# Scores and X on 32-row pieces of the array, float32 work kept together, and fewer, wider warming matmuls in an attention and two-MLP kernel

## The chip, the cores and the metric

One core of one Trainium2 chip runs the whole program. The metric is the device time of one execution in microseconds (us), the median of several runs. TensorE (PE) does the matmuls; VectorE (DVE), ScalarE (ACT) and GpSimd (POOL) do the rest; SyncE (SP) issues the DMAs. PE writes its results to PSUM, eight banks of 128 partitions x 512 float32 words.

## The reference

Four batches of eight heads, 576 tokens, 64 columns a head; the kernel unpacks the MLP weights, which come as 64-bit floats:

```python
q_lm = q.reshape(B, H, 32, 18, 64).mean(axis=3)      # 32 landmarks a head
k_lm = k.reshape(B, H, 32, 18, 64).mean(axis=3)
A  = sm(q, k_lm)          # softmax(a b^T / 8), 576 x 32
Bm = sm(q_lm, k_lm)       # 32 x 32
C  = sm(q_lm, k)          # 32 x 576
Z  = Bm^T / (norms of Bm)
for _ in range(6):
    Z = 2 * Z - Z @ Bm @ Z
x = A @ Z @ C @ v         # all heads side by side: 2304 tokens x 512
xn = x / rms(x) * rms_g
x = (silu(xn @ w_gate) * (xn @ w_val)) @ w_out       # 512 -> 1536 -> 512
out = (s * relu(x @ w_in)**2 + b) @ w_out2           # 512 -> 2048 -> 512
```

## The kernel before

**Stages.** Batch 0's attention runs first, with little beside it. Then the first MLP runs batch by batch in 12 units (blocks of 128 hidden columns, two halves of 288 tokens), and beside the units of one batch the attention of the next is computed. After the last unit and the remaining output products comes the second MLP in five blocks of up to 512 tokens.

**Precision.** The MLPs split each float32 operand into a float32r value and its remainder and add three float32r products (`PART3`; L1072, L1118, L1182, L1208 are their matmuls). The attention multiplies in float32, which leaves two records a matmul in the trace, with one exception: in batches 2 and 3 (`b >= FINE`) the scores of C and A are products of three float32r matmuls too (L707). For these, `halve` (L489) splits the transposed k or q (1152 columns) and the landmark means on ACT or DVE and DVE or POOL.

**Attention of one batch.** Heads are taken four at a time, group g = 0 or 1, a head to 32 partitions. Landmark means are sums on POOL or DVE; in batches 2 and 3 DVE transposes 32x32 blocks (L566, L596) and a product with a mask makes a block-diagonal operand of 128 columns for the four heads (L570), so that scores are matmuls over all 128 rows. Batches 0 and 1 transpose on PE (L587) and compute the scores per head on 64x32 pieces of the array (L720). `b_mm` (L620 or L615) computes B; L645 (`diag`) holds the steps of the inverse on 32x32 pieces; `c_side` and `a_side` hold the softmaxes. C's softmax finds the maximum over both halves of the row, then takes the exponentials of each (L739, L750, L755). L772 transposes C's exponentials, L794 multiplies with v. `W` = Z C v per head is written with a mask into a block operand (L859), and X = A W is computed only for the row norms: per half and group two matmuls over 64 rows each (L898), and four squares on ACT (L904). The normalised A goes to the first MLP as split operand (L944 to L950); the MLP's first weights are multiplied with W beforehand (`fused`, L1091).

**Order.** A planner written out in Python (`Scheduler`) gives every operation a due time, `key`, and lays each engine's order out from estimated durations; engines then work strictly in that order. On PE an operation has a mode, "f" or "r" (float32r); once the MLP has begun, due times in the other mode are shifted by `HOLD` or `FETCH` (L197), and a change of mode is charged (`TO_F`, `TO_R`). A batch's attention is spread by `by_path` between the times of `at_time` (L1271): from the first unit of the batch before to `EARLY` = 15 us ahead of its own first unit.

**Buffers.** PSUM banks 0 to 3 gather the output products; banks 4 to 7 (`gv_r`) serve the hidden products, and attention after batch 0 uses banks 6 and 7 of them (`at_r`). A `Buf` holds its slot from its first operation to its last.

**Warming.** Until 60 planned us, idle planned time of PE is filled with bf16 matmuls on ones, 256 columns into bank 7 (L1395), one for each `WCOST` = 0.125 us.

Of the kernel before, what the change touches and what calls it, by code (L numbers as in the profile page):

```python
# [7 lines left out]
F32 = mybir.dt.float32  # L8
# [16 lines left out]
WCOST = 0.125  # L25
FINE = 2
# [11 lines left out]
BMM = 0.15  # L38
XC = 2.0
# [9 lines left out]
HOLD, FETCH = 2.0, 4.0  # L49
AHEAD_TO, AHEAD, AHEAD_KEY = 45, 0.5, 3  # L50
# [48 lines left out]
class Scheduler:  # L99
# [48 lines left out]
    def start_of(self, o, e):  # L148
        t = max((f + (self.SAME if d == e else PEC if e == 'pe' and o.key > 5 else self.CROSS) for d, f in o.ready.items()), default=0.0)
# [17 lines left out]
    def run(self, warm):  # L167
# [8 lines left out]
        steady = False  # L176
        while left:
# [87 lines left out]
def t_act(n):  # L265
    return 0.055 + 0.00085 * n
# [15 lines left out]
def tile_nystrom_attention_two_mlps(  # L282
# [28 lines left out]
    S_ = Scheduler({"pe": nc.tensor, "dve": nc.vector, "act": nc.scalar, "pool": nc.gpsimd, "sp": nc.sync})  # L311
# [19 lines left out]
    mask4 = sb.tile([128, 1, 4, 1], F32, name="mask4")  # L331
# [30 lines left out]
    R_COLS = 15104  # L362
# [14 lines left out]
    eC_r = rring(1, 576)  # L377
# [3 lines left out]
    bd_r = rring(4, 256)  # L381
# [41 lines left out]
    def consts(_):  # L423
        nc.vector.memset(ones, 1.0)
        nc.vector.memset(spare, 1.0)
        nc.vector.memset(mask4, 0.0)
        nc.vector.memset(mask2, 0.0)
        nc.vector.memset(mask1, 0.0)
        for h in range(4):
            nc.vector.memset(mask4[32 * h:32 * h + 32, :, h, :], 1.0 / SEG)  # L430
# [26 lines left out]
    def attention(b, t0, t1):  # L457
        first = b == 0
        slow = COLD if first else 1.0
        fine = b >= FINE  # L460
        part3 = ((0, 0), (0, 1), (1, 0))
# [18 lines left out]
        area = {"t": (0, SEG * D), "bd": (SEG * D, 256)}  # L480

        def part(i, nm):
            c0, n = area[nm]
            return pair[i].t.rearrange("p k n -> p (k n)")[:, c0:c0 + n]

        def named(nm):
            return [(pair[i], nm) for i in range(2)]

        def halve(nm, x, r, n):  # L489

            wh, wl = named(nm)
            at({"act": t_act(n), "dve": t_dve2(n)}, 0, lambda e: (
                e.activation(out=part(0, nm), in_=x(), func=ACTF.Copy) if e is nc.scalar
                else e.tensor_copy(out=part(0, nm), in_=x())), r=r, w=[wh], pair=True)
            at(dp(n), 0, lambda e: e.tensor_tensor(
                out=part(1, nm), in0=x(), in1=part(0, nm).bitcast(F32), op=ALU.subtract), r=[*r, wh], w=[wl])

        src = {}
        for nm, a in (("k", k), ("q", q)):
            for g in range(2):  # L500
                t = src[nm, g] = Buf(qk_r[nm, g])

                def load_heads(e, t=t, a=a, g=g):
# [5 lines left out]
                    for h in range(4):  # L509
                        e.dma_start(  # L510
                            out=t.t[32 * h:32 * h + 32].rearrange("p (t d) -> p t d", d=D),
# [22 lines left out]
        for i, (nm, g) in enumerate((("k", 0), ("k", 1), ("q", 0), ("q", 1))):  # L534
# [19 lines left out]
            if not fine:  # L554
# [14 lines left out]
            d = bd[nm, g] = Buf(bd_r)  # L569
            at(dp(256), pos, lambda e, l=l, d=d: e.tensor_tensor(  # L570
                out=d.t.rearrange("p (e h i) -> p e h i", e=2, h=4),
                in0=l.t.rearrange("p (e o i) -> p e o i", e=2, o=1).to_broadcast([128, 2, 4, 32]),
                in1=mask4.to_broadcast([128, 2, 4, 32]), op=ALU.mult), r=[l, "const"], w=[d])

        def bdv(x):
            return x.t.rearrange("p (e m) -> p e m", e=2)

        def transposed(nm, g, pos):
# [29 lines left out]
        pB = Buf(ps_r)  # L608

        def b_mm(_):  # L610
            for g in range(2):
                if not fine:
                    for h in range(4):
                        i, p = loaded(g, h)
                        nc.tensor.matmul(  # L615
                            out=pB.t[32 * h:32 * h + 32, 32 * g:32 * g + 32], lhsT=bd["q", i].t[0:D, p],
                            rhs=bd["k", i].t[0:D, p], start=True, stop=True)
# [11 lines left out]
        def c2(x):  # L629
# [5 lines left out]
        at(("dve", t_dve(64)), pos, lambda e: e.tensor_reduce(out=bm.t[:, 0:2], in_=v2(pB), axis=AX, op=ALU.max), r=[pB], w=[bm])  # L635
        at(("dve", t_dve(64)), pos, lambda e: e.tensor_tensor(
            out=v2(Bs), in0=v2(pB), in1=c2(bm).to_broadcast([128, 2, 32]), op=ALU.subtract), r=[pB, bm], w=[Bs])
        at(("act", t_act(64)), pos, lambda e: e.activation(out=Bs.t, in_=Bs.t, func=ACTF.Exp, scale=scale / SEG if fine else scale), r=[Bs], w=[Bs])
# [62 lines left out]
        def scores(ps, nm, g, hf, p0, r, w):  # L701
            other = "kq"[nm == "k"]
            if fine:
                def mm(_):
                    for e in range(2):
                        for k, (u, y) in enumerate(part3):
                            nc.tensor.matmul(  # L707
                                out=ps.t[:, 0:HC], lhsT=part(u, "bd")[:, 128 * e:128 * e + 128],
                                rhs=part(y, "t").rearrange("p (t e i) -> p t e i", e=2, i=32)[
                                    :, HB * hf:HB * hf + HB, e, :],  # L710
                                start=(e == 0 and k == 0), stop=(e == 1 and k == 2))

                at(("pe", 6 * t_mm(HC)), p0 + 0.02, mm, r=[*named("t"), *named("bd"), *r], w=[ps, *w])
                mine[-1].mode = "r"
                return
# [11 lines left out]

        Cv = Buf(cv_r)

        def c_side(g, p0):  # L730
            for j in (g,) if fine else (0, 1) if g == 0 else ():
                transposed("k", j, p0)
# [10 lines left out]
            def in_order(hf):  # L743
                x = eC.t[:, 0:S]
                if fine:
                    return x.rearrange("p (i n) -> p n i", i=M)[:, HB * hf:HB * hf + HB]
# [18 lines left out]
            at(("dve", 0.5), p0 + 0.05, c_rec, r=[(cs, 0), (cs, 1)], w=[rc])  # L765
            pE = [Buf(ps_r), Buf(ps_r)]
# [23 lines left out]
            def cv_mm(_):  # L790
# [10 lines left out]
                e.activation(out=Cv.t[:, D * g:D * g + D], in_=pV.t[:, 0:D], func=ACTF.Copy, scale=rc.t[:, 0:1])  # L801
                if e is nc.scalar else e.tensor_scalar(
                    out=Cv.t[:, D * g:D * g + D], in0=pV.t[:, 0:D], scalar1=rc.t[:, 0:1], scalar2=None, op0=ALU.mult)),
# [3 lines left out]

        def a_side(hf, g, p0):
            if hf == 0:
                for j in (g,) if fine else (0, 1) if g == 0 else ():  # L810
                    transposed("q", j, p0)
            pA, A, a = Buf(ps_r), Buf(a_ring), Buf(AT_r)
# [10 lines left out]
            n_mine = len(mine)  # L823
# [608 lines left out]
```

## Time and profile before

| | us |
|---|---|
| median of 3 runs (lowest, highest) | 859.71 (858.71, 860.39) |
| the profiled execution's own time | 861.0 |
| its span, first to last instruction | 859.3 |
| PE busy | 843.6 |
| DVE busy | 658.2 |
| ACT busy | 460.6 |
| POOL busy | 130.0 |

Busy time is the union of an engine's instructions; matmuls overlap in the records, and their ends are modelled, so that the pace of PE is read from one start to the next. A row of the timeline gives start, duration, engine, line, tile names, shape (rows*columns of the array, then partitions x columns of the moving operand) and count.

### The profile page before, as it was taken

The page shows a single profiled execution, that of the slowest core. Times are in us where ns is not written, and L with a number is a line of the kernel's source. Part 1 is how long each engine was busy: PE and PEld are TensorE (multiplying, and loading weights), DVE is VectorE, ACT ScalarE, POOL GpSimd, SP SyncE. Part 2 cuts the span into 40 slices and gives each one's busy share as a digit, 9 for nine tenths or more (in the row PEclk, how much of TensorE's full clock was granted, in tenths as well). Part 3 has the DMA queues.
Part 4 walks back from the last instruction along what each step waited for, and adds up shares of the span by engine and source line. Part 5 has one row for each costly group of instructions (what it writes and reads, how often), then busy time and mean ns, then how long its engine had stood idle before and what let it go on. Part 6 is the DMA issues. An engine that isn't in the chain of part 4 may idle for free.

```text
span 859.3 us, 16086 instructions
## 1 busy us (share of the span) xinstructions
PE 843.6 (98%) x6039; PEld 691.4 (80%) x6039; DVE 658.2 (77%) x1492; ACT 460.6 (54%) x969; POOL 130.0 (15%) x185
## 2 busy tenths in 40 slices
PE   8899999999999999999999999999999999999997
PEld 6578776888788877888888888888888888888886
DVE  7787998889897896789978866766676667666686
ACT  5698979544544455698826633433343334333454
POOL 0270064714660143000000000000000000000000
PEclk9799999999999999999999999999999999999999
DMA  9989879644242422587732100100010001000100
GB/s 289 313 291 354 274 229 299 190 125 118 74 148 87 136 67 72 168 293 257 236 114 60 64 0 1 50 0 1 1 50 0 1 1 44 6 1 1 35 16 24
DMA packets 66493, 96.46 MB, mean 112 GB/s; under 512 B 24176, under 2 KB 44656, under 8 KB 66416
## 3 DMA queue, kind: packets, MB, share of 16 engines
q1 hardware_dynamic: 66224, 95.18, 34.9%
q8 instruction: 47, 0.77, 0.4%
q14 instruction: 30, 0.25, 0.1%
q10 hardware_dynamic: 192, 0.26, 0.1%
HBM read 81.27 MB, written 14.16 MB: 111 GB/s over the span
## 4 chain that ended last, share of the span: by engine, by line
PE 90%; DVE 4%; ACT 3%; issue 1%; DMA 0%; POOL 0%; DVEq 0%; ACTq 0%; POOLq 0%
PE bank L1208 23%; PE bank L1072 23%; PE bank L1118 17%; PE bank L1182 16%; PE bank L1091 3%; PE bank L1164 2%; PE bank L707 1%; PE bank L898 1%; PE bank L645 1%; PE bank L1395 1%; PE bank L938 1%; ACT cmag L1007 0%; DMA region<-in_k_dram 0%; PE bank L720 0%; PE bank L794 0%
## 5 line engine op out<-in xcount | busy, mean ns | idle before, releaser
L1072 PE MATMUL bank<-xh,uh 128*128 128x512 f32 (+1 forms) x320 | 119.1, 372 | 0.0
L1373 ACT ACTIVATE hbuf<-bank 128x512 f32<-128x512 f32 (+1 forms) x78 | 43.2, 553 | 141.5 <-PE bank L1072 141.4
L1072 PE MATMUL bank<-xh,ul 128*128 128x512 f32 (+1 forms) x320 | 118.8, 371 | 0.0
L1072 PE MATMUL bank<-xl,uh 128*128 128x512 f32 (+1 forms) x320 | 117.6, 368 | 0.0
L1208 PE MATMUL bank<-wh,hh 128*128 128x512 f32 x288 | 114.4, 397 | 0.3 <-DVE hh L967 0.3
L1208 PE MATMUL bank<-wl,hh 128*128 128x512 f32 x288 | 113.8, 395 | 0.0
L1208 PE MATMUL bank<-wh,hl 128*128 128x512 f32 x288 | 113.6, 395 | 0.0
L1182 PE MATMUL bank<-hh,wh 128*128 128x512 f32 (+1 forms) x224 | 87.1, 389 | 0.0
L1182 PE MATMUL bank<-hh,wl 128*128 128x512 f32 (+1 forms) x224 | 83.1, 371 | 0.0
L1182 PE MATMUL bank<-hl,wh 128*128 128x512 f32 (+1 forms) x224 | 83.0, 371 | 0.0
L968 DVE TENSOR_TENSOR hl<-hbuf,hh 128x512 fp32r<-128x512 f32 (+8 forms) x125 | 69.5, 560 | 2.8 <-ACT hh L966 0.3
L1072 PEld LDWEIGHTS bank<-xl,uh 128*128 128x128 f32 x320 | 60.3, 188 | 12.2
L1072 PEld LDWEIGHTS bank<-xh,uh 128*128 128x128 f32 x320 | 60.1, 188 | 11.5
L966 ACT ACTIVATE wh<-region 128x512 fp32r<-128x512 f32 x51 | 32.2, 631 | 69.1 <-PE bank L1208 67.9
L1072 PEld LDWEIGHTS bank<-xh,ul 128*128 128x128 f32 x320 | 60.1, 188 | 11.2
L967 DVE CAST uh<-region 128x512 fp32r<-128x512 f32 x57 | 24.3, 426 | 54.0 <-PE bank L1072 54.0
L1208 PEld LDWEIGHTS bank<-wh,hl 128*128 128x128 f32 x288 | 54.4, 189 | 13.2 <-DVE hl L968 0.2
L968 DVE TENSOR_TENSOR wl<-region,wh 128x512 fp32r<-128x512 f32 x70 | 48.5, 692 | 20.0 <-ACT wh L966 19.3
L1208 PEld LDWEIGHTS bank<-wh,hh 128*128 128x128 f32 x288 | 54.2, 188 | 11.7 <-DVE hh L967 0.7
L1208 PEld LDWEIGHTS bank<-wl,hh 128*128 128x128 f32 x288 | 54.4, 189 | 11.1
L1118 PE MATMUL bank<-xh,uh 128*128 128x288 f32 x200 | 60.7, 303 | 0.7 <-DVE hbuf L1137 0.7
L1118 PE MATMUL bank<-xl,uh 128*128 128x288 f32 x200 | 59.0, 295 | 0.0
(226 smaller groups left out, 1960.4 us busy)
## 6 DMA issues: line engine op xcount, KB each, us to landing
rawg<-keptg SPq DMA_DIRECT2D x36, 512.0 KB, 4.4
stage<-in_moe_w_out_dram SPq DMA_DIRECT2D x28, 512.0 KB, 4.8
rawo<-kepto SPq DMA_DIRECT2D x48, 256.0 KB, 2.7
stage<-in_moe_w_in_dram SPq DMA_DIRECT2D x16, 512.0 KB, 4.9
keptg<-rawg SPq DMA_DIRECT2D x12, 512.0 KB, 5.0
xbuf<-in_moe_w_val_dram SPq DMA_DIRECT2D x10, 512.0 KB, 7.4
xbuf<-in_moe_w_gate_dram SPq DMA_DIRECT2D x9, 512.0 KB, 7.0
region<-in_v_dram SPq DMA_DIRECT2D x16, 256.0 KB, 4.7
```

What stands on the lines that cost most here:

```text
L645: nc.tensor.matmul(out=ps.t[p, pn * g:pn * g + n], lhsT=lhsT(p, g), rhs=rhs(p, g), start=True, stop=True)
L707: nc.tensor.matmul(out=ps.t[:, 0:HC], lhsT=part(u, "bd")[:, 128 * e:128 * e + 128], rhs=part(y, "t").rearrange("p (t e i) -> p t e i", e=2 ...
L966: e.activation(out=hi(), in_=src(), func=ACTF.Copy) if e is nc.scalar
L967: else e.tensor_copy(out=hi(), in_=src())), r=r, w=[wh], pair=True)
L968: b = op({"dve": t_dve(n), "pool": t_pool(n)}, key, lambda e: e.tensor_tensor(out=lo(), in0=src(), in1=hi().bitcast(F32), op=ALU.subtract) ...
L1072: nc.tensor.matmul(out=ps.t[:, 0:n], lhsT=w[a].t[:, ks], rhs=x[y].t[:, kd, 0:n], start=(kd == 0 and i == 0), stop=(kd == KD - 1 and i == 2))
L1091: nc.tensor.matmul(out=pU[g].t[m, 256 * j:256 * j + 256], lhsT=gw[b].t[p, m], rhs=r.t[p, :, 128 * k:128 * k + 128], start=True, stop=True)
L1118: nc.tensor.matmul(out=ps.t[:, 0:HC], lhsT=u[a].t[:, 256 * g + 128 * part:256 * g + 128 * part + 128], rhs=x[y].t.rearrange("p k n -> p (k ...
L1164: nc.tensor.matmul(out=A[c].t[:, d:d + m], lhsT=r.t[:, 128 * c:128 * c + 128], rhs=h.t[:, o:o + m], start=f == 0 and d == 0, stop=False)
L1182: nc.tensor.matmul(out=A[c].t[:, 0:n], lhsT=w[a].t[:, 128 * c:128 * c + 128], rhs=hs[y].t[:, 0:n], start=(f == 0 and i == 0), stop=(f == F ...
L1208: nc.tensor.matmul(out=A[c].t, lhsT=hs[a].t[:, s], rhs=w[y].t, start=(f == 0 and i == 0), stop=(f == F2 - 1 and i == 2))
L1373: e.activation(out=r.t[:, 0:n], in_=ps.t[:, 0:n], func=ACTF.Relu) if e is nc.scalar
```

## The change

Scores of batches 2 and 3 (`scores2`, `c_both`, `a_side`): a call now covers both head groups of one half, with 16 float32 matmuls of 32 rows by 32 columns, two (e = 0, 1) on each of eight pieces; group 1's heads are loaded two places further round (`piece`), so that the two groups use different pieces, and each group writes its own bank. `halve` and the block-diagonal operands are gone. For k a half is 16 of the 32 segments with all their 18 tokens, not nine tokens of every segment; C's exponentials use each half's own maximum and are scaled to the common one afterwards (`fit`, one more exponential of four columns). B is computed on 32x32 pieces too, into two banks.

X of batches 1 to 3 (`XB = 1`): one call per half with eight float32 matmuls of 32 rows by 64 columns into four banks from `gv_r`; steps on a made-up engine "hold" take these banks in the planner, as each comes free, ahead of the call, and the second half's wait for the first half's call. W is copied without mask.

Planner: after a return to "r" PE stays with it for `DWELL` = 2.5 us if such work is ready (from 145 us on); attention is due 25 us instead of 15 ahead of its first unit, and that of batches 2 and 3 may begin 30 us earlier. Warming matmuls stream 512 columns (the ones read twice), one per 0.25 us.

```diff
-WCOST = 0.125
+WCOST = 0.25
+XB = 1
+SCORE2 = 1.02
+DWELL, DWELL_FROM = 2.5, 145
...
+            if e == "pe" and mode == "r" and at < since + DWELL and at > DWELL_FROM:
+                kept_r = [(t, o) for t, o in ready if o.mode == "r"]
+                if kept_r and min(t for t, _ in kept_r) <= at + self.SOON:
+                    ready = kept_r
...
                 if steady and o.mode != mode:
                     at = max(at, free[e] + (TO_R if o.mode == "r" else TO_F))
+                    since = at
...
-    eC_r = rring(1, 576)
+    eC_r = rring(2, 576)
-    bd_r = rring(4, 256)
+    bd_r = rring(4, 128)
...
+        unit = scale / SEG if b >= FINE else scale
...
+        def piece(g, h):
+
+            r = 32 * ((h + 2 * g) % 4)
+            return slice(r, r + 32)
...
-            d = bd[nm, g] = Buf(bd_r)
-            at(dp(256), pos, lambda e, l=l, d=d: e.tensor_tensor(
-                out=d.t.rearrange("p (e h i) -> p e h i", e=2, h=4),
...
-            if fine:
-                d = bd["kq"[nm == "k"], g]
-                halve("t", lambda: t.t, [t], SEG * D)
-                halve("bd", lambda: d.t, [d], 256)
...
                 for e in range(2):
-                    nc.tensor.matmul(
-                        out=pB.t[:, 32 * g:32 * g + 32], lhsT=bdv(bd["q", g])[:, e],
-                        rhs=lmT["k", g].t[:, 32 * e:32 * e + 32], start=(e == 0), stop=(e == 1))
-
-        at(("pe", 0.8 if fine else BMM), 0.18, b_mm, r=[*bd.values(), *[x for n, x in lmT.items() if n[0] == "k"]], w=[pB])
+                    for h in range(4):
+                        p, x = piece(g, h), slice(32 * e, 32 * e + 32)
+                        nc.tensor.matmul(
+                            out=pB[g].t[32 * h:32 * h + 32, 32 * g:32 * g + 32], lhsT=lmT["q", g].t[p, x],
+                            rhs=lmT["k", g].t[p, x], start=(e == 0), stop=(e == 1))
...
-            if fine:
-                def mm(_):
-                    for e in range(2):
-                        for k, (u, y) in enumerate(part3):
-                            nc.tensor.matmul(
-                                out=ps.t[:, 0:HC], lhsT=part(u, "bd")[:, 128 * e:128 * e + 128],
-                                rhs=part(y, "t").rearrange("p (t e i) -> p t e i", e=2, i=32)[
-                                    :, HB * hf:HB * hf + HB, e, :],
-                                start=(e == 0 and k == 0), stop=(e == 1 and k == 2))
...
+        def scores2(ps, nm, hf, p0, r=(), w=()):
+            other = "kq"[nm == "k"]
+
+            def mm(_):
+                for e in range(2):
+                    for g in range(2):
+                        x = tt[nm, g].t.rearrange("p (t e i) -> p t e i", e=2, i=32)
+                        x = x[:, :, e, 16 * hf:16 * hf + 16] if nm == "k" else x[:, HB * hf:HB * hf + HB, e, :]
+                        for h in range(4):
+                            p = piece(g, h)
+                            nc.tensor.matmul(
+                                out=ps[g].t[32 * h:32 * h + 32, 0:HC], lhsT=lmT[other, g].t[p, 32 * e:32 * e + 32],
+                                rhs=x[p], start=(e == 0), stop=(e == 1))
+
+            at(("pe", SCORE2), p0 + 0.02, mm, r=[*[lmT[other, g] for g in range(2)], *[tt[nm, g] for g in range(2)], *r],
+               w=[*ps, *w])
...
+        def c_both(p0):
...
+                pC = [Buf(ps_r), Buf(ps_r)]
+                scores2(pC, "k", hf, p0, [], [(x, "taken") for x in eC] if hf == 0 else [])
...
+            if fine and g == 0:
+                pA2[hf] = [Buf(ps_r), Buf(ps_r)]
+                scores2(pA2[hf], "q", hf, p0)
...
+            if b >= XB:
+                e.tensor_copy(out=WBD.t[:, 0:2 * D], in_=pW.t[:, 0:2 * D])
+                return
...
+            if b >= XB:
+                pX = [Buf(any_r if first else gv_r) for _ in range(KD)]
+                for x in pX:
+                    at(("hold", 0.0), p0, lambda e: None,
+                       r=[WBD, AT[hf, 0], AT[hf, 1]] + ([("xm", b)] if hf else []), w=[(x, "taken")])
+
+                def x_mm(_, pX=pX, hf=hf):
+                    for g in range(2):
+                        for h in range(KD):
+                            p = slice(32 * h, 32 * h + 32)
+                            nc.tensor.matmul(
+                                out=pX[h].t[D * g:D * g + D, 0:HC], lhsT=WBD.t[p, D * g:D * g + D],
+                                rhs=AT[hf, g].t[p, 0:HC], start=True, stop=True)
+
+                at(("pe", 0.65), p0, x_mm, r=[WBD, AT[hf, 0], AT[hf, 1], *[(x, "taken") for x in pX]],
+                   w=[*pX, (xq, "taken"), ("xm", b)])
...
-    EARLY = 15
+    EARLY, LEAD_B = 25, 30
...
-        return T[F1 * (b - 1)], T[F1 * b] - EARLY
+        return T[F1 * (b - 1)] - (LEAD_B if b > 1 else 0), T[F1 * b] - EARLY
...
         nc.tensor.matmul(
-            out=banks[7].t[:, 0:256], lhsT=ones.bitcast(BF16)[:, 0:128], rhs=ones.bitcast(BF16),
-            start=True, stop=True)
+            out=banks[7].t, lhsT=ones.bitcast(BF16)[:, 0:128],
+            rhs=ones.bitcast(BF16).unsqueeze(1).to_broadcast([128, 2, 256]), start=True, stop=True)
```

## Rows read from the trace of the kernel before

**Rows 1.** The page, part 1 (busy us, share, instructions) and part 3 (queue: packets, MB, share).

```profile
PE 843.6 (98%) x6039; PEld 691.4 (80%) x6039; DVE 658.2 (77%) x1492; ACT 460.6 (54%) x969; POOL 130.0 (15%) x185
...
q8 instruction: 47, 0.77, 0.4%
```

**Rows 2.** Busy time by stage: length, engines (instructions), granted clock, DMA share, GB/s.

```profile
25.00:35.00 10.00, 8.05 (x104) 4.89 (x105) 6.42 (x22) 2.93 (x8) 2.68 (x4) 0.66 1.04 372
...
55.00:420.00 365.00, 362.26 (x3392) 297.52 (x3391) 311.92 (x787) 241.17 (x557) 115.90 (x161) 1.00 0.58 188
420.00:855.00 435.00, 434.69 (x2057) 361.10 (x2055) 305.55 (x565) 182.82 (x330) 0.25 (x1) 1.00 0.09 27
```

**Rows 3.** Waits of PE: total us, times, longest.

```profile
PE bank L645 <- issue: 2.5, 1, 2.5
```

**Rows 4.** Chain that ended last, 40 to 72 us: start, us, what.

```profile
45.46 0.80 ACT cmag L1015
...
54.77 6.55 PE bank L1118 x48
```

**Rows 5.** Old scores of batches 2, 3: timeline (start, us), then one of three groups.

```profile
171.58 0.29 PE L707 MATMUL bank<-xh 128*128 128x288 f32 x1
...
172.39 0.29 PE L1118 MATMUL bank<-xh 128*128 128x288 f32 x1
...
L707 PE MATMUL bank<-xh 128*128 128x288 f32 x32 | 9.9, 311 | 0.2
```

**Rows 6.** Timeline of PE: scores of batches 0 and 1 on 64x32 pieces.

```profile
13.04 1.35 PE L720 MATMUL bank<-region 64*32 64x288 f32 x32
14.02 0.86 PE L720 MATMUL bank<-xbuf,region 64*32 64x288 f32 x16
...
98.94 0.83 PE L720 MATMUL bank<-region 64*32 64x288 f32 x16
99.70 0.50 PE L1182 MATMUL bank<-hh,wh 128*128 128x512 f32 x1
```

**Rows 7.** Timeline of PE: one call of X; group of all calls from 42 us on.

```profile
224.82 0.29 PE L1118 MATMUL bank<-xh,ul 128*128 128x288 f32 x1
225.04 0.76 PE L898 MATMUL bank<-region 64*128 64x288 f32 x4
225.72 0.40 PE L1118 MATMUL bank<-xh,uh 128*128 128x288 f32 x1
225.96 0.30 PE L1118 MATMUL bank<-xl,uh 128*128 128x288 f32 x1
226.10 0.29 PE L1118 MATMUL bank<-xh,ul 128*128 128x288 f32 x1
...
L898 PE MATMUL bank<-region 64*128 64x288 f32 x48 | 9.1, 455 | 0.0
```

**Rows 8.** Timeline of PE: B of batch 2; a short stay in the MLP.

```profile
178.88 1.08 PE L620 MATMUL bank<-region 128*128 128x32 f32 x8
...
204.39 0.33 PE L645 MATMUL bank<-region 32*32 32x32 f32 x16
204.65 0.50 PE L1182 MATMUL bank<-hh,wh 128*128 128x512 f32 x1
...
206.15 0.71 PE L772 MATMUL bank<-ident,region 128*128 128x128 f32 x5
```

**Rows 9.** ACT's work on X and on halving: min/median/max ns; then count, busy us.

```profile
L904 ACT ACTIVATE region<-bank x32: 387/408/485, 34.6 to 325.8; 128x288 f32<-128x288 f32 x32
...
L493 ACT ACTIVATE xh<-region 128x1152 fp32r<-128x1152 f32 (+1 forms) x9 | 8.9, 999 | 9.4 <-PE bank L707 8.4 <-POOL region L570 0.5 <-PE bank L1118 0.4
```

**Rows 10.** Timeline of PE: steps of batch 0's inverse with warming between.

```profile
27.96 0.65 PE L645 MATMUL bank<-region 32*32 32x64 f32 x16
28.55 1.03 PE L1395 MATMUL bank<-ones 128*128 128x256 bf16 x4
29.51 0.65 PE L645 MATMUL bank<-region 32*32 32x64 f32 x16
```

More of the change, by code (lines that the diff above doesn't have):

```diff
@@ L148, in start_of @@
     def start_of(self, o, e):
-        t = max((f + (self.SAME if d == e else PEC if e == 'pe' and o.key > 5 else self.CROSS) for d, f in o.ready.items()), default=0.0)
+        t = max((f + (0.0 if d == "hold" else self.SAME if d == e else PEC if e == 'pe' and o.key > 5 else self.CROSS) for d, f in o.ready.items()), default=0.0)
         t = max(t, o.after, self.ports if e in o.pair else 0.0)
@@ L309, in tile_nystrom_attention_two_mlps @@
     scale = 1.0 / float(D) ** 0.5
[L311 removed]
+    S_ = Scheduler({"pe": nc.tensor, "dve": nc.vector, "act": nc.scalar, "pool": nc.gpsimd, "sp": nc.sync, "hold": None})
     op = S_.op
@@ L479, in attention, with part @@
         pair = xs[1, b] = (Buf(x_r[0]), Buf(x_r[1]))
[L480 to L496, printed above, removed]
+        def part(i):
+            return pair[i].t.rearrange("p k n -> p (k n)")[:, 0:SEG * D]
+        def piece(g, h):
+            r = 32 * ((h + 2 * g) % 4)
+            return slice(r, r + 32)
         src = {}
@@ L510, in load_heads @@
                         e.dma_start(
-                            out=t.t[32 * h:32 * h + 32].rearrange("p (t d) -> p t d", d=D),
+                            out=t.t[piece(g, h)].rearrange("p (t d) -> p t d", d=D),
                             in_=a[b, 2 * h + g].rearrange("(i t) d -> i t d", t=SEG))
@@ L634, in attention, with b_max @@
         bm, bs, st, stT, nrm = (Buf(sm_r) for _ in range(5))
[L635 to L638, printed above, removed]
+        def b_max(e):
+            for g, x in enumerate(pB):
+                c = slice(g, g + 1) if fine else slice(0, 2)
+                e.tensor_reduce(out=bm.t[:, c], in_=v2(x)[:, c], axis=AX, op=ALU.max)
+                e.tensor_tensor(out=v2(Bs)[:, c], in0=v2(x)[:, c], in1=c2(bm)[:, c].to_broadcast(
+                    [128, 1 if fine else 2, 32]), op=ALU.subtract)
+        at(("dve", (0.4 if fine else 0.16) + t_dve(64)), pos, b_max, r=pB, w=[bm, Bs])
+        at(("act", t_act(64)), pos, lambda e: e.activation(out=Bs.t, in_=Bs.t, func=ACTF.Exp, scale=unit / SEG if fine else unit), r=[Bs], w=[Bs])
         at(("dve", t_dve(64)), pos, lambda e: e.tensor_reduce(out=bs.t[:, 0:2], in_=v2(Bs), axis=AX, op=ALU.add), r=[Bs], w=[bs])
@@ L730, in c_side @@
         def c_side(g, p0):
-            for j in (g,) if fine else (0, 1) if g == 0 else ():
-                transposed("k", j, p0)
+            if g == 0:
+                for j in range(2):
+                    transposed("k", j, p0)
             pC = [Buf(ps_r), Buf(ps_r)]
@@ L822, in a_side @@
             bc = [128, HB, 32]
-            n_mine = len(mine)
-            scores(pA, "q", g, hf, p0, [], [(A, "taken")])
+            if not fine:
+                scores(pA, "q", g, hf, p0, [], [(A, "taken")])
             at(("dve", t_dve(HC)), p0 + 0.03, lambda e: e.transpose(out=a3(A), in_=a3(pA)), r=[pA], w=[A])
@@ L888, in attention @@
             n_mine = len(mine)
-            for c in range(KD):
+            if b >= XB:
[4 more added lines that the diff above has]
+                def x_mm(_, pX=pX, hf=hf):
+                    for g in range(2):
+                        for h in range(KD):
[5 more added lines that the diff above has]
+                   w=[*pX, (xq, "taken"), ("xm", b)])
+                for c in range(KD):
+                    at(("act", t_act(HC)), p0 + 0.01, lambda e, c=c, pX=pX, xq=xq: e.activation(
+                        out=xq.t[:, HC * c:HC * c + HC], in_=pX[c].t[:, 0:HC], func=ACTF.Square), r=[pX[c]], w=[(xq, c)])
+            for c in range(0 if b >= XB else KD):
                 g, pr = divmod(c, 2)
@@ L954, in attention @@
                     at(("pool", 0.1), p0 + 0.11, lambda e, cols=cols: e.tensor_copy(
-                        out=mark, in_=part(1, "t")[:, cols][:, 0:1].bitcast(F32)), r=wl, w=["sums"])
+                        out=mark, in_=part(1)[:, cols][:, 0:1].bitcast(F32)), r=wl, w=["sums"])
             if hf:
```

104 lines of the change are left out of this document (71 added, 33 removed).

## The prediction

> **What bounds the kernel now.** I read the page first, then busy time by stage, then the waits of TensorE (PE), then PE's instructions in order of time. The page shows PE busy for 843.6 of 859.3 us [rows 1]. By stage the picture splits in three [rows 2]. From 420 us to the end PE is busy for 434.7 of 435 us with the second MLP, which the change does not touch: zero there. From 55 to 420 us, where the attention of batches 1 to 3 runs beside the first MLP, PE is busy 362.3 of 365 us, with VectorE (DVE) at 311.9 and ScalarE (ACT) at 241.2: a microsecond of PE work taken out here is a microsecond of time, unless a new wait appears. Before 55 us the attention of batch 0 is a chain through all engines; PE is also held 2.5 us by something that the profile calls issue [rows 3], and the granted clock averages 0.66 from 25 to 35 us, a mix of the levels 2.4 and 1.2 GHz [rows 2]. From 43 to 54 us the chain of waits lies for most of its time on ACT's unpacking of weights, and from 54.77 us on PE [rows 4].
>
> Busy times of matmuls overlap, so I price PE work by start to start.
>
> **Scores of batches 2 and 3.** Before, a call is six float32r matmuls of 288 columns on the whole array: the first starts at 171.58, the next operation's at 172.39, so 0.81 us, with no loss at either end, as the MLP uses the same mode [rows 5]. 3 x 32 matmuls [rows 5] are 16 calls: 13.0 us. After, there are 8 calls (k and q, two halves, two batches) of 16 float32 matmuls on 32x32 pieces, two per piece, on 8 different pieces. A float32 matmul leaves two records, so a call is 32 records. The trace has no such piece with 288 columns; the nearest rows are batch 0's scores on 64x32 pieces, where 8 pieces are also in use: 32 records take 13.04 to 14.02, 0.98 us [rows 6]. Inside a run of float32 work I take that. Alone, a call costs more: 16 records of the same kind that stand alone take 98.94 to 99.70, 0.76, against 0.49 inside a run, so 0.27 for the drain; and entering and leaving cost 0.08 and 0.10 (below). Alone 1.43, beside other float32 work 0.98. Half of the calls each way: 9.6 us, so **-3.4** (bounds: all beside -5.2, all alone -1.6; if only four pieces ran at a time, 0.98 more per call, +6.3).
>
> **X of batches 1 to 3.** Before, 48 records in fours are 12 calls [rows 7]. One alone: 225.04 to 225.72, 0.68; the matmul ahead of it holds PE 0.22 instead of 0.14, the first behind it 0.24 instead of 0.14: 0.86 in all [rows 7]. 12 of them: 10.3 us. After, 6 calls of 16 records on 8 pieces of 32x64. Nearest again the 16 records on 8 pieces: 0.76 alone, with 0.18 at the ends 0.94; 5.6 us, so **-4.7** (bounds: 0.49 each inside a run -7.4; four pieces at a time -1.8). The new call writes four PSUM banks, taken from the four that the first MLP uses, where the old one took two; see the first rival.
>
> **B of batches 2 and 3.** 8 records on the whole array, 1.08 us at most, become 32 on 32x32 pieces, at 0.33 for 16 [rows 8]: **-0.8** for two (bounds 0 and -1.2).
>
> **Gathering.** From 145 us on, the planner now stays with float32r work for 2.5 us after a return, as long as some is ready. In the timeline I count 40 runs of float32 work from 145 to 420 us. One alone, the 16 records of 204.39, holds PE 0.26 us, and the next starts at 206.15 after 1.5 us of MLP [rows 8]; seven runs begin less than 2.5 us behind another, apart from X's. Merging two saves the 0.18 at the ends and a drain of some 0.15 to 0.27. Four merged: **-1.4** (bounds 0 and -3).
> The Trainium skill, "TensorEngine Tiling (Array Packing)", section Tiling Modes, says that changing the tiling mode drains TensorE. It speaks against this change, which takes scores that ran in the MLP's mode out of it; the trace agrees (0.27 of drain and 0.18 at the ends), and with it every lone score call comes out at 1.43, not 0.98, which is the lower gain of 1.6 above.
>
> **Warming and the start.** 103 warming matmuls become about half as many with twice the columns, the same streaming time; where a gap has room for an odd number, one fewer. They lie on the path: between two steps of the inverse, four of them hold PE from 28.55 to 29.51, where the clock is half granted [rows 10]; the new ones would hold it as long. What can change is the 2.5 us of issue: PE stops in the middle of 16 pairs while waiting for no engine, and 6039 matmuls with as many weight loads over 47 packets of queue q8 [rows 1] are 257 per packet, so I read it as PE waiting for its code. With half the warming, some 26 pairs fewer stand ahead of it, and the shortage comes later or shorter. Bounds: +1 (two longer warming matmuls in front of a due step, at half clock), -5 (stall gone, 2.5, and the clock back for four steps of the inverse, each with half of its 0.96 of warming and some 0.1 of its matmuls, 2.3). ACT's unpacking behind it takes part of any gain [rows 4]. I take **-1.0**.
>
> **Other engines.** Gone are the halvings of k and q and of their means (ACT's casts alone 8.9 us [rows 9], and as many subtractions on DVE and GpSimd (POOL)) and the products with the block mask; new are four scalings of C per batch, one reduce, one scale and an exponential of four columns. The sum falls. Beside a PE that is the bound this is worth 0; if PE waited for this chain, it would be a gain. Attention is due 10 us earlier and may begin 30 us earlier; its loads are the same DMAs on SP's queue, which were hidden: 0.
> **New waits.** A's scores now take both attention banks at once, where a call took one and the other stayed open for the next; and PE works in order, so behind a score or X call that waits stands the MLP. For places where the new order makes PE wait I add **+1.0** (bounds 0 and +15, by the first rival).
>
> Sum: -3.4 - 4.7 - 0.8 - 1.4 - 1.0 + 1.0 = -10.3. The profiled execution took 861.0 us (span 859.3), so 850.7; the median of the runs, 859.7, is 1.3 lower: **849.4 us**.
>
> **Rivals.**
> 1. X starves the first MLP (slower). From the moment the weights are ready the new hold steps seize all four banks of the hidden layer, and the second half of the batch does the same behind the first. Until a call has run (0.94) and two squares (0.41 each [rows 9]) have freed two banks, with about 1 us of seizing ahead, no hidden matmul can run: 2.8 us. Against it: the output matmuls use other banks, and one step of them is 12 x 0.25 = 3 us [rows 8], usually ready. If none is ready, 6 x 2.8 = 17 on the sum without its +1.0: 865. It decides against the change from an idle time of 11.3 / 6 = 1.9 us per call.
> [...]
> 2. Only four pieces run side by side: +6.3 for the scores, -1.8 for X, B 0, the rest as above: +3.1, 862.8. Rows 6 speak against it, but with 64-row pieces.
> 3. Nothing is gathered: scores all alone (-1.6) and no run fewer (0): -7.1, 852.6. The count of float32 runs would show it.
> 4. The code stall and the low clock go altogether: 4 more, 845.4.
> 5. The waiting for float32r work strings out the attention chain, and PE stands at the start of batches 2 and 3, 3 us each: 855.4. Against it: the chain is given 10 us more lead.
>
> **Chances.** Forecast 0.52 (its own range 846 to 852), rivals 0.10, 0.04, 0.14, 0.12, 0.08. The range that leaves out 2 in 10 runs from 844.5 to 857.5. A measurement here can tell 0.2%, 1.7 us, from none. Faster by more: forecast and rivals 3 to 5 less their tails, 0.84; slower: rivals 1 and 2 less theirs, 0.11; within: 0.05.
>
> **What would show it.** Right: one call of the new scores at 1.0 to 1.45 us start to start and X at 0.5 to 0.95; fewer than 40 float32 runs between 145 us and the end of the first MLP; that end about 10 us earlier; the second MLP as long as before. Wrong: PE idle beside X with its squares as releaser (rival 1); records of a call at 60 ns apart (rival 2); a PE wait at a batch's first hidden matmul (rival 5). A start phase that is shorter by more than 2 us would mean rival 4; one that is longer by more than 1 us, that my reading of the warming is wrong.

## The result, and the profile after

The changed kernel takes **851.85 us** (median of 6 runs, 850.33 to 853.25) against 858.59 for the kernel before on the same chip: a ratio of 0.9915, 95% interval 0.9898 to 0.9932. The profiled execution took 850.33 us, its span is 848.6. Forecast were 849.4, between 844.5 and 857.5. The time falls as forecast; several terms of the sum, and the idea that they add, don't hold.

The page of the changed kernel, parts 1 and 3, to compare with [rows 1]: PE is busy 12.3 us less, the span is 10.7 shorter.

```profile
PE 831.3 (98%) x6241; PEld 670.5 (79%) x6241; DVE 648.2 (76%) x1469; ACT 454.8 (54%) x971; POOL 118.3 (14%) x172
...
q8 instruction: 49, 0.80, 0.4%
```

Busy time by stage, after, with the columns of [rows 2] and borders moved by the 10.5 us by which the second MLP starts earlier (433.2 before, 422.7 after). The clock from 25 to 35 us is full instead of 0.66 (in a second profile of the same kernel, r2, it is 0.66 from 25 to 30 us and full from there); the middle still leaves PE 3.7 us without work; the last stage is as it was.

```profile
25.00:35.00 10.00, 8.45 (x118) 4.20 (x117) 9.53 (x28) 6.50 (x16) 2.93 (x5) 1.00 1.07 375
...
55.00:410.00 355.00, 351.27 (x3626) 281.83 (x3625) 297.56 (x763) 231.78 (x550) 98.47 (x144) 1.00 0.61 189
410.00:844.00 434.00, 433.70 (x2053) 360.21 (x2051) 304.86 (x564) 182.18 (x329) 0.25 (x1) 1.00 0.10 27
```

Waits of PE, after: the stop of 2.5 us at the inverse [rows 3] is gone, and waits for the hidden layer's gating on DVE (L1227, before L1137: the product that follows the tanh) have grown, over all of PE's lines from 1.8 to 4.0 us. The waits of the hidden matmuls among them, after and then before:

```profile
PE bank L1208 <- DVE hbuf L1227: 1.9, 2, 1.2
...
PE bank L638 <- issue: 0.2, 1, 0.2
```

```profile
PE bank L1118 <- DVE hbuf L1137: 0.7, 1, 0.7
```

The timeline of PE, after: one call of the new scores, of the new X and of the new B, each with the matmul ahead of it and behind it, to compare with [rows 5, 7, 8].

```profile
162.94 0.39 PE L1272 MATMUL bank<-hh,wl 128*128 128x512 f32 x1
163.25 1.20 PE L718 MATMUL bank<-region 32*32 32x288 f32 x32
164.38 0.40 PE L1208 MATMUL bank<-xh,xh 128*128 128x288 f32 x1
164.62 0.29 PE L1208 MATMUL bank<-xl,xh 128*128 128x288 f32 x1
...
225.40 0.40 PE L1272 MATMUL bank<-hh,wl 128*128 128x512 f32 x1
225.73 0.74 PE L970 MATMUL bank<-region 32*64 32x288 f32 x16
226.40 0.50 PE L1272 MATMUL bank<-hh,wh 128*128 128x512 f32 x1
226.73 0.39 PE L1272 MATMUL bank<-hl,wh 128*128 128x512 f32 x1
...
251.47 0.38 PE L607 MATMUL bank<-region 32*32 32x32 f32 x32
251.78 0.50 PE L1272 MATMUL bank<-hh,wh 128*128 128x512 f32 x1
```

A score call takes 1.13 us start to start (163.25 to 164.38), X 0.67, B 0.31.

All comparisons below split a profiled execution at the first hidden matmul. What lies ahead of it is **the start**; the span without it is **the rest**. A kernel's rest repeats within 0.2 us from profile to profile (before 814.4 and 814.6, after 809.1 and 809.1); the start moves by 1 us. So the medians say whether a kernel is faster, and the rest says where edits below half a per cent go. The border is read from the group of the first hidden matmuls (min/median/max ns, then first start to last start); after:

```profile
L1208 PE MATMUL bank<-xh,uh x200: 288/295/512, 39.5 to 416.7; 128*128 128x288 f32 x100
```

### The profile page after: what moved, and what is told of

It reads as the page before. It is cut to its first block, busy times and chain, and to the rows that moved or that the text cites. A ratio compares the mean times of both kernels' runs of the same rounds, so it can differ in the third digit from the quotient of the medians.

```text
span 848.6 us, 16465 instructions
## 1 busy us (share of the span) xinstructions
PE 831.3 (98%) x6241; PEld 670.5 (79%) x6241; DVE 648.2 (76%) x1469; ACT 454.8 (54%) x971; POOL 118.3 (14%) x172
## 4 chain that ended last, share of the span: by engine, by line
PE 82%; DVE 2%; ACT 1%; POOL 1%; issue 0%; POOLq 0%; DVEq 0%
PE bank L1298 24%; PE bank L1162 23%; PE bank L1272 15%; PE bank L1208 14%; PE bank L1181 2%; PE bank L718 1%; PE bank L638 1%; PE bank L1028 0%; POOL region L547 0%; POOL region L543 0%; PE bank L970 0%; PE bank L1007 0%; DVE wl L1058 0%; DVE region L998 0%; ACT region L977 0%; PE bank L832 0%
## 5 line engine op out<-in xcount | busy, mean ns | idle before, releaser
L1058 DVE TENSOR_TENSOR hl<-hbuf,hh 128x512 fp32r<-128x512 f32 (+8 forms) x130 | 73.9, 572 | 3.3 <-ACT hh L1056 0.7
```

The lines of the kernel that those rows point to most:

```text
L1058: b = op({"dve": t_dve(n), "pool": t_pool(n)}, key, lambda e: e.tensor_tensor(out=lo(), in0=src(), in1=hi().bitcast(F32), op=ALU.subtract) ...
```

## Experiments

Each row below is a median with its count of runs, the ratio to the kernel before on the same chip with its 95% interval, then from the profile the start, the rest, and the length of the units of batches 0, 1 and 2 (first hidden matmul to first hidden matmul of the next batch, hidden matmuls being counted off in the timeline).

```
                      median (n)   ratio [95%]              start  rest   b0    b1    b2
before                859.9  (17)  1                        44.9  814.4  107.5 101.2  99.8
after                 851.85 (6)   0.9915 [0.9898, 0.9932]  39.5  809.1  110.2  98.5  94.7
r1 before again       859.76 (11)  1.0    [0.9989, 1.0012]  43.7  814.6  107.6 101.2  99.8
r2 after again        851.49 (4)   0.991  [0.9897, 0.9924]  40.6  809.1  110.2  98.5  94.7
r3 after, old warming 854.83 (5)   0.9942 [0.9928, 0.9956]  46.0  808.6  109.7  98.5  94.7
r4 before, new warm.  857.20 (7)   0.9971 [0.996, 0.9981]   41.5  814.4  107.9 101.2  99.8
r5 no stay            851.75 (6)   0.991  [0.9893, 0.9928]  39.8  810.2  110.2  97.3  97.1
r6 old due times      867.69 (6)   1.0092 [1.007, 1.0114]   39.7  825.4  116.0 107.8  99.0
r7 old X              858.85 (12)  0.9994 [0.9981, 1.0007]  39.8  815.4  111.3 100.3  98.0
r8 scores alone       862.73 (12)  1.0031 [1.0018, 1.0045]  46.1  815.7  108.1 103.4  98.6
r9 old due, no stay   861.05 (12)  1.0026 [1.0009, 1.0042]  39.9  817.5  114.6  99.6  97.6
r10 old scores        868.61 (4)   1.0114 [1.0096, 1.0132]  40.2  827.3  106.7 116.8  98.0
r11 warming padded    854.34 (6)   0.9954 [0.9936, 0.9971]  42.6  808.8  109.9  98.5  94.7
r12 batch 1 as before 863.79 (7)   1.0053 [1.0034, 1.0071]  41.1  823.1  109.4 103.8 103.7
```

**r1 and r2: the two kernels again**, with no edit.

> The kernel before, unchanged, timed against itself. It shows what the comparison can tell, and gives a second profile of a kernel whose first profiled execution (861.0 us) lay 2.4 us above the median of its six runs (858.59). Theory: the difference between executions is made ahead of 55 us (the 2.5 us stop of PE and the clock at its lower level behind it), so a profile near 857 to 859 shows the stop shorter or the clock higher there and the same times from stage to stage after about 95 us. Rival: executions differ all along the first MLP. Time within 1.5 us of 858.6 in either case.

> The changed kernel, unchanged. Expected 851 to 853 us, ratio 0.990 to 0.994. Its first profiled execution (850.3) kept the full clock from 4.6 us on and started the first MLP at 39.5 us. Theory: at 852 or more the profile shows a stop of PE or a stretch of lower clock ahead of 45 us again, and from 95 us on the same stage lengths as in the first profile (batch 1 to 2 98.5 us, 2 to 3 94.7 us).

The gain repeats: 859.91 to 851.49, 8.4 us. The first profiles had shown 10.7 us; some 2 of those were the two starts (44.9 was a long one, 39.5 a short one).

**r3 and r4: the old warming in the kernel after, the new one in the kernel before.**

```diff
-WCOST = 0.25
+WCOST = 0.125
...
-            out=banks[7].t, lhsT=ones.bitcast(BF16)[:, 0:128],
-            rhs=ones.bitcast(BF16).unsqueeze(1).to_broadcast([128, 2, 256]), start=True, stop=True)
+            out=banks[7].t[:, 0:256], lhsT=ones.bitcast(BF16)[:, 0:128], rhs=ones.bitcast(BF16),
+            start=True, stop=True)
```

> The changed kernel with the old warming matmuls (256 columns, one per 0.125 us), all else as changed. Theory: the shorter start of the profiled execution (first hidden matmul at 39.5 instead of 44.9 us) is taken back by ACT's unpacking before 95 us (half of batch 0's units at 93.5 instead of 94.5), so the warming is worth 0 to 1.5 us: 852 to 853.5. Rival: the start is the main gain, and without the new warming 855 to 857. If PE's stop is a wait for code, it returns here: 1 to 3 us of issue around 24 us.

> The kernel before with the new warming alone (512 columns, one per 0.25 us). Theory: 857 to 858.6, that is 0 to 1.5 us faster, with the first hidden matmul 2 to 5 us earlier and most of that gone by the middle of batch 0's units. Rival, the start as the main gain: 853 to 855.

The old warming costs the kernel after 3.3 us (854.83 against 851.49), the new one gives the kernel before 2.7 (857.20 against 859.91), and the rest moves by 0.5 us at most. The timeline of PE in r3, step of the inverse: PE stops in the middle of 16 matmuls for 2.88 us with no engine awaited.

```profile
24.65 0.26 PE L638 MATMUL bank<-region 32*32 32x32 f32 x7
27.79 0.33 PE L638 MATMUL bank<-region 32*32 32x32 f32 x9 [2.88 <-issue]
```

The same step in the kernel after runs through:

```profile
24.61 0.33 PE L638 MATMUL bank<-region 32*32 32x32 f32 x16
24.86 0.39 PE L1485 MATMUL bank<-ones 128*128 128x512 bf16 x1
```

Busy time by stage in r3 (columns of [rows 2]): around the stop and behind it the clock is at 0.75 and 0.56, where the kernel after has 1.00 twice in its first profile and 0.66, then 1.00 in its second.

```profile
25.00:30.00 5.00, 2.21 (x32) 1.31 (x31) 1.97 (x7) 2.75 (x6) 1.63 (x3) 0.75 1.06 393
30.00:35.00 5.00, 5.00 (x67) 2.79 (x65) 4.06 (x15) 0.25 (x2) 1.34 (x2) 0.56 1.08 360
```

**r11: the count of PE's instructions as before, the wide warming kept.** A matmul of one column stands behind each warming matmul of 512.

```diff
+        nc.tensor.matmul(
+            out=banks[7].t[:, 0:1], lhsT=ones.bitcast(BF16)[:, 0:128], rhs=ones.bitcast(BF16)[:, 0:1],
+            start=True, stop=True)
```

> The changed kernel with a warming matmul of one column behind each of 512 columns: about 98 warming pairs on PE instead of 49, as many as before the change, with the new streaming time. Theory, PE's stop at 24 us is a wait for its code, set by the number of instructions: the stop of 1 to 3 us with issue as releaser comes back, and the first hidden matmul at 43 to 46 us; 854 to 856. Rival, the width of the warming or its timing does it: no stop, first hidden matmul at 40 to 42 us, 851 to 852.5.

The stop is back, in the same step (timeline of PE, r11), and the first hidden matmul comes at 42.6 instead of 39.5 and 40.6:

```profile
24.57 0.31 PE L638 MATMUL bank<-region 32*32 32x32 f32 x10
27.16 0.26 PE L638 MATMUL bank<-region 32*32 32x32 f32 x6 [2.28 <-issue]
```

So the stop hangs on how many instructions PE has ahead of that point, not on the columns streamed: all five profiles with the old count (before, r1, r3, r8, r11) have a stop of 2.2 to 2.9 us with no engine awaited, and none of the nine with the new warming has one of over 0.2. The gain of the warming goes with it: the ratio is 0.9954, for 0.991 in r2 and 0.9942 in r3. The start comes back only in part (46.0 in r3).

**r5: no stay in float32r** (PE may return to float32 work at once).

```diff
-DWELL, DWELL_FROM = 2.5, 145
+DWELL, DWELL_FROM = 0.0, 145
```

> The changed kernel with the stay in float32r work at 0 instead of 2.5 us, all else as changed (851.5). In the changed kernel I count 42 runs of float32 work from 145 us to the end of the first MLP, against 40 before. Theory: the gathering has replaced the runs that the scores add (8) less those that X saves (4); without it some 4 to 8 runs more at 0.3 us each: 853 to 854. Rival: it brings nothing, or strings out the chain: 850.5 to 852.

The rest grows by 1.1 us; the medians can't tell (851.75 against 851.49 and 851.85). Batch 1's units get shorter without it (97.3), batch 2's longer (97.1). Counted in the timeline between the first hidden matmul and the middle of batch 3's units, the stay makes 62 float32 runs of 69 (a run is float32 work with no float32r matmul between).

**r6 and r9: due times as before, with the stay and without it.**

```diff
-    EARLY, LEAD_B = 25, 30
+    EARLY, LEAD_B = 15, 0
```

and for r9 `DWELL` 0.0 too.

> The changed kernel with the old due times of attention (15 us ahead, no earlier beginning for batches 2 and 3). The changed kernel needs 110.2 us for batch 0's units where the one before needs 107.5, with 4.9 against 2.7 us of PE waits there, though its X is 2 us cheaper. Theory: the earlier due time of batch 1's attention, with ACT and DVE both over 90% busy there, makes these waits; with the old due times batch 0's stage falls to 106 or less and the sum by 1 to 4 us (847.5 to 850.5). Rival: the earlier attention is what lets batches 2 and 3 run without waits; then they get longer by more: 852 to 856.

> The changed kernel with the old due times (15 us ahead, no earlier beginning) and no stay in float32r work; new scores, X and warming. With the stay, the old due times cost 16 us (867.7), 11 us of it PE waits. Theory: it is the stay that strings out the attention chain, so that it comes late where it has no lead; without the stay 850 to 853. Rival: X, which seizes the hidden layer's four banks, starves it when its time comes close to the batch's start; then 860 to 868 without the stay too.

Without the earlier due time the kernel is slower than before, where both theories had it faster. Of the rest's 16.3 us (r6) the stay makes 7.9: r9 has 8.4. The timeline of PE in r6, then DVE's: batch 3's B (L607) takes both attention banks at 254.79, while batch 2's attention is not yet done; DVE reduces them only at 258.47 (L626), as a transpose of 1.4 us, the splitting of fused weights and a weight's remainder stand ahead of that in its order. PE's next product of batch 2's attention (L1028) stands 3.81 us for the banks, and no hidden or output matmul lies in PE's order between 254.79 and the first hidden matmul of batch 2 at 263.47.

```profile
253.24 0.59 PE L1007 MATMUL bank<-ones,region 128*96 128x1 f32 x6
253.76 1.09 PE L1181 MATMUL bank<-rawg,gw 64*32 64x256 f32 x32
254.79 0.43 PE L607 MATMUL bank<-region 32*32 32x32 f32 x32
259.02 2.26 PE L1028 MATMUL bank<-region,ones 96*128 96x288 f32 x4 [3.81 <-DVE region L626]
261.21 1.96 PE L1181 MATMUL bank<-rawg,gw 64*32 64x256 f32 x32
263.10 0.44 PE L638 MATMUL bank<-region 32*32 32x32 f32 x16
263.47 0.54 PE L1208 MATMUL bank<-xh,uh 128*128 128x288 f32 x1
```

```profile
254.32 1.38 DVE L585 STREAM_TRANSPOSE region<-region 128x1152 f32<-128x1152 f32 x1
255.62 0.71 DVE L1194 CAST uh<-bank 128x256 fp32r<-128x256 f32 x2
256.46 1.42 DVE L1196 TENSOR_TENSOR ul<-bank,uh 128x256 fp32r<-128x256 f32 x4
257.80 0.76 DVE L1058 TENSOR_TENSOR wl<-rawo,wh 128x512 fp32r<-128x512 f32 x1
258.47 0.18 DVE L626 TENSOR_REDUCE region<-bank 128x1 f32<-128x32 f32 x1
```

So 8.7 us pass at one place without the MLP's matmuls: PE stands for 3.81 of them and does most of the rest at a lower clock. The same 32 records of L1181 hold PE 1.03 us ahead of the stand (253.76 to 254.79) and 1.89 behind it (261.21 to 263.10). The clock of the stretch (0.57, so mostly the lower of the two levels):

```profile
256.00:264.00 8.00, 4.97 (x55) 2.68 (x56) 6.23 (x23) 4.80 (x11) 2.88 (x5) 0.57 0.45 166
```

In r9 no wait of PE is longer than 1.6 us; of the 8.4 us of its rest 4.4 lie in batch 0's units (114.6), 1.1 in batch 1's and 2.9 in batch 2's.

**r7: X as before.**

```diff
-XB = 1
+XB = 4
```

> The changed kernel with the old X (two matmuls over 64 rows, two banks) in all batches. The new call measures 0.67 us alone, so 6 x 0.85 = 5.1 us with its ends, against 10.3 for the old. Theory: all of it on the path, so 4 to 5.5 us slower: 855.5 to 857. Rival, four banks starve the hidden layer and take part of it back: 852 to 854.

Nearly the whole gain goes: 858.85, the rest 6.3 us longer. The 12 old calls hold 8.28 us against 4.02 for six new ones; 70 float32 runs instead of 62 may be part of what is above these 4.3.

**r8: the scores, B and the softmax alone** (old warming, old X, no stay, old due times: the diffs of r3, r5, r6 and r7 together).

> The scores, B and the softmax of C as changed, and nothing else: old X, old warming, no stay, old due times. Against the kernel before (859.9). Eight score calls measure 1.13 us each in the changed kernel, 1.31 with their ends, against 0.81 for 16: 2.5 us saved, and 0.5 to 0.8 for B. Theory: 856.5 to 857.5. Rival: without gathering the planner strings out the float32 work and the gain is gone: 859 to 861.

Slower than before by 0.31%, where even the rival had at most 861. The calls themselves are as cheap as in the kernel after (9.18 us for eight, 13.5 for the sixteen of before), but there are 76 float32 runs for 64, and PE's waits between the first hidden matmul and the middle of batch 3's units are 8.2 us for 4.4. The largest ones in r8 (us in total, times, longest):

```profile
PE bank L638 <- DVE region L683: 1.5, 2, 1.0
PE bank L1028 <- DVE hbuf L1227: 1.4, 1, 1.4
```

**r10: everything but the scores.** The kernel before, with its halving, float32r scores, B and softmax, and X, warming, stay and due times of the kernel after.

```diff
-WCOST = 0.125
+WCOST = 0.25
+XB = 1
+DWELL, DWELL_FROM = 2.5, 145
...
-    EARLY = 15
+    EARLY, LEAD_B = 25, 30
```

> The changed kernel with the scores, B and C's softmax of the kernel before (float32r on the whole array, k and q halved); new X, warming, stay and due times. The scores alone on top of the kernel before made the part behind the first hidden matmul 1.2 us longer (815.7 against 814.4), though their matmuls take 9.0 us instead of 12.9. Theory: beside X and the stay the new scores gain the 2 to 3 us that their matmuls save, so this one takes 853 to 855. Rival: they gain nothing at all, what their matmuls save goes into waits and changes of mode: 849 to 852.

868.61: the slowest of all, and outside both of the expected ranges. Batch 1's units alone take 18.3 us more (116.8 for 98.5). Busy time by stage, r10, the units of batch 1 cut in two; then its largest wait of PE there.

```profile
147.00:208.00 61.00, 57.53 (x603) 48.35 (x602) 53.29 (x137) 30.35 (x77) 27.85 (x40) 1.00 0.57 165
208.00:263.70 55.70, 48.78 (x369) 37.99 (x368) 39.67 (x96) 22.00 (x50) 22.11 (x31) 0.91 0.26 82
```

```profile
PE bank L1148 <- DVE hbuf L1167: 4.3, 4, 1.8
```

The kernel after, the same units:

```profile
149.70:199.40 49.70, 48.47 (x582) 38.44 (x582) 38.23 (x110) 21.23 (x63) 15.60 (x23) 1.00 0.49 148
199.40:248.20 48.80, 48.40 (x465) 39.54 (x463) 39.90 (x99) 24.44 (x65) 20.20 (x29) 1.00 0.42 125
```

With old scores DVE (third pair) is busy 53.3 of the first 61 us and 93.0 over the batch, with the new ones 38.2 of 49.7 and 78.1. PE waits 10.1 us in the batch instead of 1.6. The waits for the gating (L1167) lie in the second part, from 210.8 to 241.8, where DVE is busy 39.7 of 55.7 us, while four of the five large halvings on DVE lie in the first; so it is not shown that DVE's load alone makes PE wait. The clock at 0.91 in the second part puts some 10 of its 55.7 us at the lower level. By my count from the first hidden matmul to the middle of batch 3's units PE's waits are 14.7 us in r10 and 6.6 in the kernel after.

**r12: a mixture.** Batch 1's attention as before (old X, due 15 us ahead), the rest as after.

```diff
-XB = 1
+XB = 2
...
-        return T[F1 * (b - 1)] - (LEAD_B if b > 1 else 0), T[F1 * b] - EARLY
+        return T[F1 * (b - 1)] - (LEAD_B if b > 1 else 0), T[F1 * b] - (EARLY if b > 1 else 15)
```

> The changed kernel, but with batch 1's attention as before: the old X (two banks) and 15 us of lead in batch 1, the new X and the new due times in batches 2 and 3. Batch 0's units, beside which batch 1's attention runs, took 110.2 us in the changed kernel, 107.6 before and 108.0 with the new scores alone. Theory: the new X and due time bring nothing in batch 1, whose stage is held by waits on DVE, so this stage takes 107.5 to 108.5 and the sum 849 to 850. Rival: the new due times belong together; batch 2's earlier start then collides with batch 1's later end, and the stage takes 112 or more: 853 or more.

It was to take back the 2.7 us by which batch 0's units are longer after the change. It took back 0.8 (109.4), and batches 1 and 2, whose operations are the same as in the kernel after, lose 5.3 and 9.0. The timeline of PE in r12 shows its longest wait, in batch 1's units, 15 us ahead of the first hidden matmul of batch 2: behind batch 3's B (L607) a hidden matmul stands 2.00 us for the remainder of its fused weights (L1196). That is one place; the 14.0 us of the rest are not accounted for by it.

```profile
236.48 0.33 PE L607 MATMUL bank<-region 32*32 32x32 f32 x16
...
239.35 0.40 PE L1208 MATMUL bank<-xh,xh 128*128 128x288 f32 x1 [2.00 <-DVE xl L1196]
```

No variant beats the changed kernel.

## Why the prediction was right, and where it was wrong

PE work between the first hidden matmul and the middle of batch 3's units, the same 1008 hidden and 435 output matmuls in both, counted start to start: 348.0 us before, 342.8 after.

- **Scores, -3.4: right as a price.** The sixteen old calls held 13.5 us, the eight new ones 9.03. The call shown loses 0.08 ahead (163.25 less 162.94 and a usual 0.23) and 0.10 behind (0.24 for 0.14): 1.4 for eight, so -3.1. Eight pieces do run side by side: rival 2 (2.1 us a call) is out. The agreement is in part luck: half of the calls were to stand beside other float32 work at 0.98, and none does so at both ends (six of the eight stand alone, all eight hold PE 1.13); a lone call, forecast at 1.43 with its ends, takes only 1.31. **Wrong as a gain:** alone they make the kernel slower (r8), and in company they are worth 18.2 us of the rest (r10 against after). My "other engines: 0" named a possible reason and dropped it ("if PE waited for this chain, it would be a gain"): 15 us of DVE's work go in batch 1's units, and where they stay PE waits 8.5 us more there. That the one makes the other, or is all of the 18.2, is not shown.
- **X, -4.7: the calls right, the worth larger.** Six calls hold 4.02 us for 8.23; with six pairs of ends saved, at 0.18 each, -5.3. Undone, the rest grows by 6.3 (r7). Rival 1 did not come about: PE waits for the squares of X once, for 0.2 us. But a shortage of banks is real in r6, in the *attention's* two, both of which the new B takes: 3.8 us.
- **B, -0.8: a little small**, 0.67 for 1.83, so -1.2.
- **Gathering, -1.4: wrong in how it shows, about right in size.** I forecast fewer than 40 runs of float32 after 145 us; there are 42. What the stay does is undo the splitting that the new pieces bring (69 runs without it, 62 with it, 64 before): 1.1 us against r5, nothing against the kernel before.
- **Warming and the start, -1.0: right in kind, a third in size.** It is worth 2.7 (r4) to 3.3 us (r3). Rival 4, the stop and the low clock gone altogether, is what the first profile shows (1.00 from 25 to 35 us); r2 has 3.4 us at the lower level still. I had given the rival 4 us more than the forecast and a chance of 0.12; measured, it is worth 2 more. The step of this term that failed is "ACT's unpacking behind it takes part of any gain": the middle of batch 0's units is reached at 93.5 after and at 99.5 in r3, so that the 6.5 us of earlier start in these two profiles are all still there but 0.5.
- **New waits, +1.0: too small.** PE's waits in the stretch go from 4.4 to 6.6 us; the places are L1227's gating (above), not the score calls that seize two banks.
- **Other engines, due times, DMAs, 0: the step that failed.** Old due times make it 867.69 (r6), old scores 868.61 (r10). The 25 us are no detail of the planner: without them the kernel loses more than the whole change gains. The stay shows it most plainly: it gains 1.1 us with the early due time (r5) and loses 7.9 with the old one (r6 against r9). Rival 5, waiting for float32r work strings out the attention chain, fits that loss, and the lead keeps it out of the kernel after. X points the same way: with the early due time and the stay the new X gains 6.3 us; with the old one and no stay it loses 1.8 (r9's 817.5 against r8's 815.7, which differ in the warming too, worth 0.5 of the rest at most).

Scores, X and B came to -9.6 where -8.9 were forecast, but the rest fell only by 5.3. By what each operation holds PE, start to start, the difference lies in the hidden matmuls (145.2 us for 141.0, with the waits behind them; the output products give 1.4 back) and in fused weights and transposes (+0.9 and +0.7); 2.2 of it are waits. The stages show the same: batch 0's units +2.7, batch 1's -2.7, batch 2's -5.1. The first half of batch 0's units is the longer one, after then before:

```profile
39.50:93.50 54.00, 51.11 (x502) 38.97 (x500) 45.72 (x115) 50.69 (x103) 16.99 (x22) 1.00 1.03 342
```

```profile
44.90:94.50 49.60, 47.81 (x442) 37.16 (x441) 40.11 (x103) 45.89 (x91) 15.89 (x21) 1.00 0.97 337
```

More of the attention's work lies in it (60 more records of PE, 12 more instructions of DVE), the second half gives back 1.7. So the forecast of 849.4 came near 851.85 in part by luck, as two errors of opposite sign met: the rest was to fall by 9.3 us and fell by 5.3, and the start was to gain 1.0 and gained about 3.

The Trainium skill, "TensorEngine Tiling (Array Packing)", section Tiling Modes, has a change of the tiling mode drain TensorE. The trace agrees with a price: behind the call shown the next hidden matmul takes 0.24 instead of 0.14 start to start, ahead of it the output product 0.31 instead of 0.23. It is small here: what the switches cost is less than what a new order of the same work costs (r6: 16.3 us).

**Open.** No run has the new due times alone on the kernel before, or the old scores with the new due times and nothing else, so the price of the lead by itself is unknown, and r10 does not say with which of X, stay and due times the old scores clash. Why each order of the planner comes out as it does: an edit to one batch changes the others (r12), so 2.7 us in batch 0's units and 8.4 in r9 are located, not explained. How the 2.7 to 3.3 us of the warming divide between the stop (2.2 to 2.9 in the kernels that have it) and the clock was not separated; neither was why the stop lasts as long as it does.

## What to carry to other kernels

In a kernel whose order a planner lays out from due times, price the edits of PE by the row, but don't add them up as if they were independent: here scores, X and stay each lose with the old due time (1.3, 1.8 and 7.9 us of the rest), and together with the new one they take 5.3 us off it. Ask of every engine that you book at 0 in which half of a stage it is nearly full, and try the lead that the new order needs together with the edit, not after it. A stop of PE that waits for no engine, in the middle of equal matmuls, can be tried by changing the number of instructions ahead of it.

## What the runs showed of the hardware that was not expected

- Half as many warming instructions on PE, with the same columns, take away a stop of 2.2 to 2.9 us that waits for no engine; one-column matmuls that only restore the count bring it back (r11: 2.28 us in the same step). The clock does not follow the stop alone: it is at 0.79 from 25 to 30 us in r11, and at 0.66 in r2, r4 and r10, which have no stop. The row of r11:

```profile
25.00:30.00 5.00, 2.84 (x45) 1.42 (x45) 2.57 (x10) 2.94 (x6) 1.87 (x4) 0.79 1.05 387
```

- Float32 matmuls on eight 32x32 pieces keep the pace of the 64x32 pieces: 32 records of 288 columns in 1.13 us alone, where the forecast had 0.98 to 1.25 from [rows 6]; 16 on 32x64 pieces take 0.67 against 0.76.
- Pieces that take different rows can write one PSUM bank side by side, if each writes partitions of its own. A score call writes two banks, each from four such pieces (`scores2`). If a bank took one piece at a time, each bank's 16 records would go one by one in the 1.13 us, 0.07 us each; the four records of an old X call, of as many columns, take 0.68 (225.04 to 225.72), at least twice that each.
- A stand of PE of 3.8 us costs more than itself: in r6 the granted clock is 0.73 during it (255.2 to 259.0) and 0.50, the lower level, from 259 to 263, just where the chain to the next batch's first hidden matmul has nothing beside it.
